# A gated linear attention block and a gated MLP on one core: the decay of the state once per 128 tokens instead of once per 64, its transport through device memory, a broadcast load of the bias, and a new order of steps

## The chip, the cores and the metric

The kernel runs on one core of a Trainium2 chip. The metric is device time in microseconds (us) from launch to end, as the median of several executions. The engines of the core work side by side, each through its own list of instructions in order: TensorE (PE; its weight loads are the row PEld), VectorE (DVE), ScalarE (ACT), GpSimd (POOL), and SyncE (SP), which here only issues DMAs.

## The reference

B = 4 batches, H = 8 heads, S = 768 tokens, D = 48 features a head. First a linear attention whose state decays by a gate per feature, then an MLP with spatial gating over the tokens and a residual:

```
f = sigmoid(f_logit)
for t in range(S):
    state = f[t][:, None] * state + outer(k[t], v[t])      # per batch and head, 48 x 48
    y[t]  = q[t] @ state
x = y as (B, S, 384)
h = gelu(x @ w_in)                 # 1024 columns: u is the first 512, v the last 512
v_n = (v - mean) / sqrt(var + 1e-6) * g_ln
v_s = einsum('ts,bsd->btd', w_sg, v_n) + b_sg[:, None]
out = x + (u * v_s) @ w_out
```

## The kernel before

The tokens are cut into 24 tiles n of 128 tokens, six to a batch. Inside a tile the attention works in two chunks of C = 64 tokens. With c the running sum of log f from the start of the chunk, the kernel scales q by exp(c) (step `mq`) and k by exp(-c) (`mk`); the scores of a chunk are then a masked product of the two, and the state is carried from chunk to chunk in scaled form. After each chunk the new products are added to the state (`sa`, `state_add`) and the sum is multiplied by the whole decay of the chunk, exp(c) of its last token (`sm`, `state_mul`). That decay stands along tokens-by-features and is wanted with features on partitions, so it has to be turned. For the six tiles of the first batch PE turns it (`do`, `dec_pick`, L544: eight small matmuls, which pick rows 63 and 127 of exp(c)), and DVE or ACT copies it out of PSUM (`di`, `dec_take`). For tiles 6 to 23 it goes through device memory: one DMA writes the two rows to `dec_d` (`do`, L532), two DMAs read them back, one for even heads and one for odd ones (`di`, L536), each element on its own partition.

The names of a tile's steps: `f`, `q`, `k`, `v` load inputs; `e`, `l` make log f on ACT; `cum` sums it with a triangular matrix (`tril`, L507, fp32, for the first batch; L510 and L511 in two fp32r parts after that); `up`, `dn` are the two exponentials; `tr` turns q and k with PE (L559, first batch), later tiles are turned by DVE and device memory (`tt`, `to`, `ti`); `tc` copies them; `w` copies v rows; `su` (`scores`, L604 scores and L609 state products, pair of heads by pair of heads); `ms` masks; `y` (L652) makes the output; `ty`, `jy` take it from PSUM; `xT` (L681), `xh`, `xl` turn and split x in a high and a low half; `hv` and `hu` are the products with w_in; `gv`, `ns` ... `nl` are gelu and the norm of v, whose split halves are `vh` and `vh_lo`; `sg` is the product over tokens with w_sg; `sb`, `sm_`, `sh`, `sl` add the bias, gate and split; `po` is the product with w_out; `re`, `out` add x and store. Every large product is three fp32r matmuls (high by high, high by low, low by high), all on L676. The weights arrive as float64 and are decoded in seven steps, `wa` to `wf` (one `ldin` or `ldout` load, then work on ACT, DVE and POOL); w_sg is turned by `wT` (L436).

The bias b_sg is one row of 768 numbers that every partition needs. Before, it is loaded to one partition (`b`), spread over 128 by two matmuls with a row of ones (`bb`, L909), and copied by ACT (`bc`) to `b_bc`.

What runs when is written out by hand: `ORDER` lists all steps, with an engine where there is a choice. A planner (`Plan.run`) walks the list with the costs in `T` and `W` to give every step a buffer, a PSUM bank and a planned start; on each engine the order is that of the list. Matmuls on zeros (L1054, `Plan.warm`) are put where the planner sees PE idle before 45 us, to keep its clock up.

Of the kernel before, what the change touches and what calls it, by code (L numbers as in the profile page):

```python
# [76 lines left out]
wT2.1 hv2 wh2.1 waout3 tc4.1 w4.0:ACT tc4.0 mq5:POOL w3.0:POOL wrin2 nl1 mk5 sa3.1 wcin2 wl2.1 y3 su4 ty3 gv2 wein0
sm3.1:POOL sa4.0 wpout3 ns2 tr5 bb1 do5 ldin3 ldsg0 ldout1 tc5.0:DVE ms4 tc5.1:DVE e6 jy3 di5 wfin1:POOL sm4.0:POOL
wfin0:POOL hu0.1 xT3 wT0.0 nd2 w4.1:POOL w5.1:POOL wdin2 sa4.1 wein2:DVE bc1 l6 lh6 wain3 y4 su5 wT0.1 xh3 w5.0:ACT
nd0 nq0 wh0.0 wqout3 wfin2 wpin3 xl3 wqin3 ms5 wh0.1 nq2 ty4 wl0.0 wl0.1 nr0 sm4.1:POOL nh0:DVE wrout3 sa5.0 jy4  # L80
waout1 gu0.1 sm5.0:POOL nr2 wpout1 nl0 hu0.2 hv3 xT4 y5 wT1.1 gu0.2 gv3 xh4 ty5 nh2 wh1.1 hu0.0 wqout1 wcout3 ll6
wrin3 jy5 xl4 ns3 wcin3 wdout3 xT5 hv4 nd3 xh5 nq3 q7 f7 ldout2 f8 ldout0 k7 wl1.1 xl5 wdin3:POOL sz6 nr3 hu1.0 hv5
nl2 waout2 gv4 wein3 wrout1 wcout1 wdout1 ns4 wfin3 weout3:DVE nd4:DVE nh3 nl3 weout1 v8 ldsg5 ldsg4 v6 v7 k6 q8 f9 q6
ldsg3 w8.0:ACT gv5 hu1.2 wfout1 wpout2 wqout2 ns5 nd5:DVE nq4 gu1.0 nr4 hu1.1 cum6 nq5 gu0.0 gu1.2 nr5 wfout3 wrout2
wcout2 nh4:DVE wdout2 nh5:DVE nl5 weout2:DVE nl4 gu1.1 up6 dn6 e7 l7 lh7 hu1.3 hu0.3 sg0.0 wT4.0 mk6 tt6.0 mq6 tt6.1
wfout2 ll7:POOL zr gu0.3 gu1.3 wh4.0 f10 to6 do6 cum7 sg0.2 wl4.0 sb0.0 sm_0.0 sb0.2 up7 dn7 e8 e9 ti6.0 ti6.2 ti6.3
ti6.1 k8 wT3.1 wT5.0 wT3.0 mq7:POOL mk7:POOL sg0.3 wh3.1 wh5.0 l8 wh3.0 lh8 wl3.1 tt7.0 tt7.1 wl5.0 wl3.0 sm_0.2:POOL
ll8:POOL cum8 wT4.1 wT5.1 l9 tc6.1 waout0 up8 dn8 lh9 sh0.2:DVE tc6.0:DVE sb0.3 sl0.2 wpout0 wqout0 ll9:POOL su6 wh5.1
wh4.1 sg0.1 ms6 wl4.1 mk8 wrout0 mq8 wl5.1 wcout0 cum9 di6.1 f11 di6.0 do7 to7 di7.1 ti7.2 di7.0 ti7.3 e11 up9 e10 dn9
l10 sh0.0 lh10 wdout0:POOL sb0.1 sa6.0 sm_0.1 weout0:DVE tt8.0 tt8.1 f12 ti7.1 k9 do8 ti7.0 q9 to8 sg1.0 sg1.2  # L90
wfout0:POOL mk9 sm6.0 sa6.1 ll10:POOL l11 sh0.1 tc7.1 sm_0.3 tc7.0:DVE sm6.1:POOL sl0.1 w6.0 sh0.3 w7.0:ACT w6.1:ACT
cum10 su7 y6 sl0.3 sl0.0 f13 di8.0 ti8.0 ti8.2 ti8.1 ti8.3 tt9.0 sb1.0 lh11 e13 ty6 up10 dn10 tc8.0 e12 tc8.1
ll11:POOL mq9:POOL jy6 tt9.1 sb1.2 ms7 sa7.0 sm7.0 w7.1 sa7.1 po1 po0 k10 to9 q10 di8.1 do9 v9 xT6 su8 y7 sm7.1 re0
xh6 ty7 po2 cum11 out0 ti9.3 di9.0 ti9.2 ti9.1 ti9.0 xl6 mk10 tt10.0 mq10:POOL jy7 sm_1.2 up11 sh1.2 ms8 sa8.0 tt10.1
sm8.0 w8.1:ACT w9.1:ACT dn11 sa8.1 re1 tc9.1:DVE sl1.2 sm_1.0 l12 tc9.0 hv6 xT7 y8 su9 k11 to10 q11 v10 ti10.1 di9.1
do10 k12 q12 f14 xh7 ty8 gv6 lh12 sh1.0:DVE mk11 sl1.0 ll12:POOL re2 jy8 xl7 tt11.0 mq11 sg1.1 xT8 cum12 sg1.3 xh8 l13
# [1077 lines left out]
```

## Time and profile before

| what | value |
|---|---|
| runs | 360.13, 360.68, 362.65 us; median 360.68 |
| span of the profiled execution | 358.9 us |
| outside the span, median less span | 1.8 us |
| granted TensorE clock, mean | 0.996 of full speed |
| busy: PE, PEld, DVE, ACT, POOL | 351.7, 322.9, 243.5, 213.7, 98.9 us |

The span runs from the first to the last instruction of the profiled execution, whose own time outside the profiler is not recorded; the median of the runs is 1.8 us above the span. Engine busy times overlap with one another. The ends of matmuls are modelled, so a PE that is shown as busy all the time may still have room; PEld, the weight loads, is a second witness.

### The profile page before, as it was taken

The numbers are of one execution on the slowest core, as the hardware profiler recorded it, in microseconds if no ns is written. First come the engines' busy times: TensorE is split into PE (matmuls) and PEld (weight loads), VectorE is DVE, ScalarE is ACT, GpSimd is POOL, SyncE is SP. The second block draws the span as 40 slices with busy tenths as digits, with TensorE's granted clock in tenths as the row PEclk, the third lists the DMA queues.
The fourth block names the chain that finished last, engine by engine and source line by source line (L and its number), as shares of the span: only waits on it lengthen the run. The fifth ranks groups of instructions, "written<-read, shape, count | busy, mean of one in ns | idle before, by whom it ended". The sixth has DMA issues, their size and how long they took to land.

```text
span 358.9 us, 11336 instructions
## 1 busy us (share of the span) xinstructions
PE 351.7 (98%) x4664; PEld 322.9 (90%) x4664; DVE 243.5 (68%) x553; ACT 213.7 (60%) x469; POOL 98.9 (28%) x158
## 2 busy tenths in 40 slices
PE   8999999999999999999999999999999999999994
PEld 3778788999999899999999999999998998999993
DVE  4888889969899956666655778457667665324551
ACT  5688799896737896996355758485226463701000
POOL 3433534243511140234122222114124121201210
PEclk9999999999999999999999999999999999999998
DMA  8999947955767867766357452742264440010012
GB/s 185 220 188 265 186 132 179 210 158 112 185 157 173 190 167 154 165 149 140 80 133 182 78 154 57 200 79 75 81 112 112 121 106 2 2 66 2 0 44 96
DMA packets 133903, 45.74 MB, mean 127 GB/s; under 512 B 117205, under 2 KB 130261, under 8 KB 133846
## 3 DMA queue, kind: packets, MB, share of 16 engines
q1 hardware_dynamic: 133846, 44.96, 55.0%
q8 instruction: 38, 0.62, 0.8%
q14 instruction: 19, 0.16, 0.1%
HBM read 33.09 MB, written 11.85 MB: 125 GB/s over the span
## 4 chain that ended last, share of the span: by engine, by line
PE 87%; DMA 5%; DVE 3%; SPq 2%; ACT 1%; issue 1%
PE ps_b L676 65%; PE ps_y L652 6%; PE ps_s L604 4%; DMA raw<-kq_d 3%; PE ps_s L609 2%; PE ps_b L681 2%; PE ps_b L559 2%; PE ps_b L544 1%; PE ps_b L436 1%; PE ps_b L1054 1%; DMA kq_d<-gg 1%; DMA gg<-in_moe_w_in_dram 1%; PE ps_b L507 1%; PE ps_b L510 1%; PE ps_b L511 1%
## 5 line engine op out<-in xcount | busy, mean ns | idle before, releaser
L676 PE MATMUL ps_b<-w_sg_hi,vh 128*128 128x384 f32 x192 | 65.6, 342 | 0.0
L676 PE MATMUL ps_b<-w_sg_hi,vh_lo 128*128 128x384 f32 x192 | 64.8, 338 | 0.0
L676 PE MATMUL ps_b<-w_sg_lo,vh 128*128 128x384 f32 x192 | 64.8, 338 | 0.0
L676 PE MATMUL ps_b<-w_out_hi,gg 128*128 128x384 f32 x174 | 48.2, 340 | 0.0
L769 DVE SCALAR_TENSOR_TENSOR tmp<-ps_b,cols,b_bc 128x384 f32<-128x384 f32 x32 | 19.4, 610 | 24.9 <-PE ps_b L676 24.7
L676 PEld LDWEIGHTS ps_b<-w_sg_hi,vh 128*128 128x128 f32 x192 | 36.0, 188 | 0.3
L676 PEld LDWEIGHTS ps_b<-w_sg_lo,vh 128*128 128x128 f32 x192 | 36.1, 188 | 0.0
L676 PEld LDWEIGHTS ps_b<-w_sg_hi,vh_lo 128*128 128x128 f32 x192 | 36.0, 188 | 0.0
L297 ACT ACT_TABLE_LOAD x27 | 34.6, 1283 | 0.5
L676 PEld LDWEIGHTS ps_b<-w_out_hi,gg 128*128 128x128 f32 x174 | 31.7, 188 | 0.3
L676 PE MATMUL ps_b<-w_out_lo,gg 128*128 128x384 f32 x87 | 29.1, 335 | 0.0
L676 PE MATMUL ps_b<-xTh,w_in_hi 128*128 128x384 f32 x84 | 29.0, 345 | 0.0
L676 PE MATMUL ps_b<-xTl,w_in_hi 128*128 128x384 f32 x84 | 28.4, 338 | 0.0
L676 PE MATMUL ps_b<-xTh,w_in_lo 128*128 128x384 f32 x84 | 28.4, 338 | 0.0
L652 PEld LDWEIGHTS ps_y<-vs,st 64*64 64x64 f32 x768 | 24.4, 134 | 4.2 <-issue 2.4
L774 POOL TENSOR_TENSOR tmp<-tmp,u 128x384 f32<-128x384 f32 x13 | 14.1, 1088 | 49.6 <-DVE tmp L769 37.2
L652 PE MATMUL ps_y<-vs,st 64*64 64x48 f32 x768 | 27.1, 219 | 0.0
L652 PE MATMUL ps_y<-S,sk 48*64 48x48 f32 x768 | 27.0, 219 | 0.0
L299 ACT ACTIVATE f<-f 128x384 f32<-128x384 f32 x48 | 25.1, 524 | 2.1 <-DMA f<-in_f_logit_dram 1.7
L676 PE MATMUL ps_b<-w_in_hi,xTh 128*128 128x512 f32 x63 | 25.5, 405 | 0.0
L633 POOL TENSOR_TENSOR S<-S,dec 112x192 f32<-112x192 f32 x22 | 12.5, 570 | 45.8 <-DVE S L630 34.2
L604 PEld LDWEIGHTS ps_s<-sk 48*64 48x64 f32 x768 | 20.8, 133 | 4.8 <-issue 2.1
(150 smaller groups left out, 889.7 us busy)
## 6 DMA issues: line engine op xcount, KB each, us to landing
kq_d<-gg SPq DMA_DIRECT2D x18, 384.0 KB, 2.5
f<-in_f_logit_dram SPq DMA_DIRECT2D x24, 192.0 KB, 3.5
kq<-in_q_dram SPq DMA_DIRECT2D x24, 192.0 KB, 4.3
kq<-in_k_dram SPq DMA_DIRECT2D x24, 192.0 KB, 4.1
vs<-in_v_dram SPq DMA_DIRECT2D x24, 192.0 KB, 4.5
raw<-kq_d SPq DMA_DIRECT2D x36, 128.0 KB, 2.5
out_dram<-tmp SPq DMA_DIRECT2D x24, 192.0 KB, 1.8
gg<-in_moe_w_in_dram SPq DMA_DIRECT2D x8, 384.0 KB, 5.5
```

What stands on the lines that cost most here:

```text
L297: nc.scalar.preload_act_table_set(SETS[want])
L299: nc.scalar.activation(dst, src, func, **kw)
L436: nc.tensor.transpose(ps[:, j], t[:, (hf * KT + j) * P : (hf * KT + j + 1) * P], ident)
L559: nc.tensor.transpose(psum[f"tr{n}"][j][:W2, p * P : (p + 1) * P], kq[:, j, 2 * p : 2 * p + 2, :].rearrange("t h d -> t (h d)")[:, :W2], i ...
L604: nc.tensor.matmul(ps_s[rows(score_rows(c, 2 * p + par)), par, p * C : (p + 1) * C], sk[r, 0, p, c], sk[r, 1, p, c], start=True, stop=True)
L609: nc.tensor.matmul(ps_s[feat(par), c, 256 + p * D : 256 + (p + 1) * D], kt[rows(c), h], vs[rows(c), h], start=True, stop=True)
L633: ENG[e].tensor_mul(state_to(n, c), state_to(n, c), decay(n, c))
L652: nc.tensor.matmul(ps_y[rows(c), half, h * D : (h + 1) * D], a, m, start=start, stop=stop)
L676: nc.tensor.matmul(ps, a, m, start=(j == 0), stop=(j == len(seq) - 1))
L681: nc.tensor.transpose(ps[:, j], x_sb[n][:, j * P : (j + 1) * P], ident)
L769: nc.vector.scalar_tensor_tensor(t, psum[f"sg{g}.{ft}"][:, :E], g_col[:, ft : ft + 1], b_bc[:, tokens(g)], op0=ALU.mult, op1=ALU.add)
L774: ENG[e].tensor_mul(t, t, uT.pop((g, ft)))
```

## The change

- The running sum starts anew only with each 128-token tile: the line that cleared the block of `tril` between the chunks is gone. exp(c) and exp(-c) now reach over 128 tokens.
- The state of chunk 0 is not decayed any more: `sa` of the first chunk adds (or, for a batch's first tile, copies), `sa` of the second adds, and one `sm` a tile multiplies. 40 multiplications become 20, as the last tile of a batch needs none. `y` of tile n waits for `sa` n.0 and `sm` n-1.
- The decay of a tile is one row of 384 numbers. All 24 tiles send it through device memory: `do` is one DMA, `di` two, with 4 instead of 8 numbers per partition. The PE steps `do` of tiles 0 to 5 and their copies are gone, and 18 DMAs come in their place on SP.
- The bias is loaded by one DMA that reads the row for each of 128 partitions; `bb`, `bc` and the row of ones are gone.
- `scores` makes the scores of three pairs of heads, their state products, then the scores and state products of the fourth, instead of alternating pair by pair.
- `ORDER` and the costs `T`, `W` are redone, with other choices of engine; due times, which nothing read, are gone.

```diff
-        pool.memset(tril[:C, C:], 0.0)
...
-        nc.gpsimd.memset(dec[:, NT:], 1.0)
+        nc.gpsimd.memset(dec, 1.0)
...
     def dec_out(n, e):
-        ENG[e].dma_start(dec_d[n].rearrange("c (h d) -> c h d", d=D), eb_of[n][C - 1 :: C, :, 0:D])
+        ENG[e].dma_start(dec_d[n : n + 1].rearrange("c (h d) -> c h d", d=D), eb_of[n][P - 1 : P])
     def dec_in(n, par, e):
-        ENG[e].dma_start(
-            dec[feat(par), n].rearrange("d c p -> d (c p)"),
-            dec_d[n].rearrange("c (p x d) -> x d (c p)", x=2, d=D)[par],
-        )
-    def dec_pick(n):
...
-    def dec_take(n, e):
...
+        ENG[e].dma_start(dec[feat(par), n], dec_d[n].rearrange("(p x d) -> x d p", x=2, d=D)[par])
...
+        for some in (range(NP - 1), range(NP - 1, NP)):
+            for p in some:
+                pair_scores(p)
+            for p in some:
+                pair_state(p)
...
-    def state_add(n, c):
+    def state_add(n, c, e):
         if n % NT == 0 and c == 0:
-            nc.vector.tensor_mul(state_to(n, c), U(n, c), decay(n, c))
+            copy(e, state_to(n, c), U(n, c))
         else:
             nc.vector.tensor_add(state_to(n, c), Sts[n % 2][:W2, c], U(n, c))
-    def state_mul(n, c, e):
-        ENG[e].tensor_mul(state_to(n, c), state_to(n, c), decay(n, c))
+    def state_mul(n, e):
+        ENG[e].tensor_mul(state_to(n, 1), state_to(n, 1), dec[:, n, :, None].to_broadcast((W2, NP, D)))
...
-    dma("b", lambda e: nc.sync.dma_start(b_bc[0:1], b_sg[None, :]), W["b"], ["f5"], due=35.0)
-    op("one", lambda e: nc.gpsimd.memset(one, 1.0), T["one"], ())
-    for g in range(2):
-        pe(f"bb{g}", lambda g=g: b_rows(g), T["bb"], ["b", "one"], due=40.0)
-        op(f"bc{g}", lambda e, g=g: copy(e, b_bc[:, tokens(g)], psum[f"bb{g}"][:, :E]), T["bc"], [f"bb{g}"], unbank=f"bb{g}")
+    dma("b", lambda e: nc.sync.dma_start(b_bc, b_sg[None, :].to_broadcast((P, S))), W["b"], ["f5"])
...
+        dma(f"do{n}", lambda e, n=n: dec_out(n, e), W["do"], [f"up{n}", f"mq{n}"], free=[("eb", f"up{n}", 0)])
+        for par in range(2):
+            dma(f"di{n}.{par}", lambda e, n=n, par=par: dec_in(n, par, e), W["di"], [f"do{n}", "clear"])
```

The start of `ORDER`, up to the first `hv`, before (-) and after (+):

```diff
-f0 ldin6 ldin1 cs clear f1 q0 k0 e0 l0 wain6 zy zs wpin6 wqin6 v0 q1 k1 ldin4 ldin7 v1 f2 cum0 f3 wain1 up0 dn0 e1
-wrin6 wpin1 wcin6 wqin1 wdin6 wein6 l1 mq0:POOL one wrin1 mk0 wcin1 cum1 tr0 up1 tc0.1 dn1 w0.0 tc0.0:DVE wain4
-w0.1:ACT wdin1:POOL wain7 do0 su0 mq1 wfin6:POOL ldin5 q2 k2 ms0 di0 sa0.0 sm0.0 mk1:POOL sz0 do1 tr1 sa0.1 sm0.1
-wpin4 wqin4 wrin4 di1:ACT tc1.0 tc1.1 y0 su1 w1.0:ACT e2 w1.1:ACT l2 ty0 e3 l3 wpin7 wcin4 wqin7 wrin7 wdin4 f4 q3 f5
-v2 k3 sa1.0 wcin7 jy0 ms1 sm1.0:POOL cum2 cum3 wdin7:POOL wain5 wpin5 wqin5 up2 up3 dn2 dn3 y1 xT0 ty1 xh0 e4 mq2
-wrin5 mk2 do2 wcin5 jy1 xl0 di2:ACT l4 mq3 tr2 xT1 wein7 tc2.1 xh1 e5 wdin5:POOL cum4 do3 tc2.0:DVE sa1.1 wein5 l5 up4
-di3:ACT su2 cum5 v3 ldin0 ldsg2 b ldsg1 q4 ldin2 q5 k4 ldout3 wfin7:POOL sm1.1:POOL w2.0:ACT w2.1:ACT dn4 xl1 cum_c
-wein4:DVE wfin5 mk3 wfin4 tr3 hv1 tc3.0 tc3.1 wain0 up5 dn5 gv1 ms2 sa2.0 sm2.0:POOL sa2.1 wpin0 sm2.1:POOL wqin0
...
+f0 cs ldin6 f1 clear e0 zy ldin7 ldin4 l0 wain6 wpin6 e1 l1 q0 cum_c wain7 wain4 k0 wqin6 ldin5 wrin6 cum0 wpin7 wcin6
+up0 wqin7 wpin4 dn0 zs mk0 f2 v0 wain5 wdin6 mq0:POOL wein6 wrin7 wqin4 do0 q1 wpin5 k1 wqin5 wrin5 wrin4 wcin7 wcin5
+cum1 tr0 e2 tc0.0 tc0.1 su0 l2 wcin4 cum2 up1 wdin5 mq1 v1 f3 wein5:DVE di0.0 di0.1 dn1 up2 f4 w1.1:ACT sa0.0 sa0.1
+wdin7 ms0 ldin1 w0.0:ACT mk1:POOL w0.1:POOL wdin4 tr1 tc1.0 sz0 do1 y0 wein4:DVE tc1.1 wfin5 k2 e3 q2 w1.0 ty0 sm0 q3
+zr su1 e4 jy0 l3 dn2 wain1 ms1 l4 xT0 sa1.0 wpin1 wein7:DVE mk2 wqin1 cum3 mq2 y1 up3 cum4 wfin6:POOL dn3 xh0 ty1 tr2
+wfin7 di1.1 v2 xl0 jy1 mq3:POOL di1.0 xT1 wrin1 tc2.1 tc2.0 f5 k3 do2 sa1.1 xh1 xl1 e5 ldin0 wfin4:POOL w2.1:POOL do3
+wcin1 up4 ldsg2 l5 su2 hv1 dn4 wain0 w2.0:POOL cum5 sm1 sa2.0 v3 ldsg1 mk3 ms2 up5 sa2.1 q4 dn5 tr3 y2 k4 tc3.0
...
```

After the first `hv` the list before goes on with `su3 y2`, two `wT`, `hv0 bb0 xT2 do4 tr4` ... to `hu1.3 hu0.3 sg0.0`; the list after with `su3`, two `wT`, `hv0 tr4 xT2` ... to `hu1.2 sg0.0 hu1.3` (PE steps only).

## Rows read from the trace of the kernel before

**Rows 1.** The page, head and busy time by engine (us, share, instructions).

```profile
span 358.9 us, 11336 instructions
...
PE 351.7 (98%) x4664; PEld 322.9 (90%) x4664; DVE 243.5 (68%) x553; ACT 213.7 (60%) x469; POOL 98.9 (28%) x158
```

**Rows 2.** Windows: length; busy PE, PEld, DVE, ACT, POOL (instructions); granted clock, DMA share, GB/s.

```profile
0.00:10.00 10.00, 8.43 (x17) 3.49 (x18) 4.59 (x12) 5.72 (x12) 4.46 (x20) 1.00 0.94 185
10.00:70.00 60.00, 59.56 (x1025) 49.88 (x1026) 53.91 (x129) 49.40 (x119) 24.21 (x40) 1.00 0.92 198
...
100.00:350.00 250.00, 249.70 (x3252) 236.89 (x3251) 159.03 (x360) 135.31 (x287) 57.47 (x87) 1.00 0.46 106
```

**Rows 3.** Chain that ended last, 0 to 60 us: start, us, what.

```profile
9.89 0.91 PE ps_b L507 x2
...
11.69 0.69 PE ps_b L544 x8
...
13.46 0.42 PE ps_b L1054 x2
...
27.69 0.54 PE ps_b L1054 x2
...
28.50 0.09 PE ps_s L609 x8
28.59 0.13 PE ps_s L604 x8
...
29.25 0.84 PE ps_b L507 x2
30.09 0.87 PE ps_b L559 x8
30.96 2.09 PE ps_b L676 x9
...
37.90 0.84 PE ps_b L909 x2
...
47.43 0.88 PE ps_b L544 x8
```

**Rows 4.** The same chain, its end.

```profile
353.88 0.56 DVE tmp L800
```

**Rows 5.** Timeline of DVE: first weight step, last weight step ahead of the first h matmuls.

```profile
5.79 0.36 DVE L394 TENSOR_SCALAR u<-u 128x384 uint32<-128x384 uint32 x1 [3.46 <-ACT u L389]
...
29.25 0.55 DVE L427 TENSOR_TENSOR w_in_lo<-u,w_in_hi 128x384 fp32r<-128x384 f32 x1
```

**Rows 6.** Timeline of DVE: the last low half of the first batch.

```profile
71.42 0.75 DVE L742 SCALAR_TENSOR_TENSOR vh_lo<-vg,vg_rs,vh 128x512 fp32r<-128x512 f32 x1
```

**Rows 7.** Timeline of PE: the first spatial matmuls, and the first that reads token tile 4.

```profile
72.78 0.34 PE L676 MATMUL ps_b<-w_sg_hi,vh 128*128 128x384 f32 x1
...
74.89 0.34 PE L676 MATMUL ps_b<-w_sg_hi,vh 128*128 128x384 f32 x1
```

**Rows 8.** Groups by line: busy us, mean ns, idle before and its releaser.

```profile
L633 POOL TENSOR_TENSOR S<-S,dec 112x192 f32<-112x192 f32 x22 | 12.5, 570 | 45.8 <-DVE S L630 34.2 <-ACT f L299 5.7 <-DMA dec<-dec_d 5.1
...
L633 DVE TENSOR_TENSOR S<-S,dec 112x192 f32<-112x192 f32 x18 | 7.5, 419 | 1.4 <-DMA dec<-dec_d 1.1
...
L676 PEld LDWEIGHTS ps_b<-w_in_hi,w_sg_hi 128*128 128x128 f32 x18 | 3.4, 188 | 0.7
```

**Rows 9.** DMA of the page: share of the queue; issues, KB each, us to landing.

```profile
q1 hardware_dynamic: 133846, 44.96, 55.0%
...
gg<-in_moe_w_in_dram SPq DMA_DIRECT2D x8, 384.0 KB, 5.5
```

**Rows 10.** Instructions on the tile dec: ns min/median/max; its DMAs.

```profile
L536 SPq DMA_DIRECT2D dec<-dec_d x36: 302/470/1525, 79.2 to 290.5; - x36
...
DMA to landing us min/median/max: 2.0/2.4/3.3
```

**Rows 11.** Waits of SP's queue: total, times, longest.

```profile
SPq L536 <- DMA dec_d<-eb: 7.9, 5, 2.5
```

More of the change, by code (lines that the diff above doesn't have):

```diff
@@ L77 @@
[L77 to L96, printed above, removed]
@@ L142 @@
-sm_6.1:POOL sh6.1:DVE sl6.3 sl6.1 sb6.0 sm_6.0:POOL sm_6.2 sh6.0:DVE sl6.0 sh6.2 sl6.2 sb7.3 sb7.2 sm_7.3 sm_7.2:POOL
-sh7.3 sl7.3 sh7.2:DVE sl7.2 po18 po19 po21 re19 ok re18 out18 out19 po20 po22 ok_s re20 ok_e re21 re22 po23 out20
-out21 out22 re23 hold out23
+f0 cs ldin6 f1 clear e0 zy ldin7 ldin4 l0 wain6 wpin6 e1 l1 q0 cum_c wain7 wain4 k0 wqin6 ldin5 wrin6 cum0 wpin7 wcin6
+up0 wqin7 wpin4 dn0 zs mk0 f2 v0 wain5 wdin6 mq0:POOL wein6 wrin7 wqin4 do0 q1 wpin5 k1 wqin5 wrin5 wrin4 wcin7 wcin5
@@ new lines @@
+nr5 wl0.1 k8 q8 nh5:DVE l7 up6 dn6 nl5 wcout2 ldsg3 e8 mq6 wdout2 e9 mk6 l8 lh7:DVE hu0.3 weout2:DVE ldsg5 hu1.1 tt6.0
+f10 gu0.3 wfout3:POOL hu1.2 tt6.1 ll7 sg0.0 hu1.3 sb0.0 gu1.1 wT3.0 w8.1:ACT gu1.2 cum7 lh8:DVE wfout2:POOL wT3.1
+gu1.3 up7 wh3.0 dn7 sm_0.0:POOL do6 ll8 to6 ti6.1 wh3.1 w7.0 mq7 mk7:POOL wl3.0 ti6.2 e10 di6.0 ti6.3 wl3.1 sg0.2 l9
+wT4.0 sb0.2 cum8 sg0.3 wh4.0 up8 ti6.0 wT5.1 tt7.0 f11 sm_0.2:POOL dn8 lh9 di6.1 di5.1 sh0.0 tt7.1 mq8 to7 waout0
+wT5.0 ll9:POOL do7 tc6.0 tc6.1 wh5.0 e11 wl4.0 wpout0 mk8 wqout0 f12 l10 sb0.3 ti7.0 wT4.1 ti7.1 wl5.0 tt8.0 ti7.3
@@ new lines @@
+wh5.1 sm_0.3:POOL l11 wrout0 tt8.1 wh4.1 ti7.2 wcout0 do8 su6 w7.1:ACT w6.0:ACT cum9 to8 lh10 wdout0 sa6.0 wl5.1
+ll10:POOL sh0.3 sa6.1 ms6 sg0.1 sh0.2 di7.0 k9 tc7.1 up9 wl4.1 q9 tc7.0 cum10 y6 weout0:DVE ti8.0 lh11:DVE e12 su7
+sm6:POOL ti8.1 sl0.3 ll11 sl0.0 sb0.1 wfout0 mq9:POOL q10 v9 ms7 cum11 dn9 mk9:POOL ty6 jy6 l12 lh12 tt9.0 ti8.2 k10
+do9 sm_0.1 f13 ti8.3 di8.1 up10 dn10 sa7.0 ll12:POOL sg1.0 w8.0:ACT tt9.1 sh0.1 di7.1 xT6 w9.1:ACT sl0.2 sl0.1
+mq10:POOL up11 sb1.0 to9 xh6 sa7.1 sm_1.0 e13 di9.1 dn11 tc8.1 mk10 do10 tc8.0:DVE di9.0 f14 ti9.3 e14 ti9.0 ti9.1
@@ L145 @@
+nl23 hu7.2 hu7.0 hu7.1 gu7.1 hu7.3 gu7.0 ok sg7.1 sg6.2 gu7.2 sb6.2 sg6.1 sg7.3 sb7.1 sb6.1 sm_6.1:POOL sm_6.2:POOL
+sh6.2:DVE sm_7.1 sh7.1 gu7.3 sg6.0 sg7.2 sg6.3 sh6.1 sl6.1 sl7.1 sb7.3 sl6.2 sb6.0 sg7.0 sm_7.3 sm_6.0 sh6.0:DVE sh7.3
+sb7.2 sl6.0 sb6.3 sm_6.3 sh6.3 sl6.3 sb7.0 sm_7.0 sm_7.2:POOL sh7.0 sl7.0 sl7.3 sh7.2:DVE sl7.2 po18 po19 po21 po20
+re18 re19 out19 ok_s out18 re20 po22 out20 po23 ok_e re21 re22 re23 out22 out21 out23 hold
 """
@@ L333, in gla_moe_kernel @@
     Sts = [cp.tile([P, 2, NP, D], F32, name=f"S{i}") for i in range(2)]
-    ebs = [cp.tile([P, H, HD], F32, name=f"eb{i}") for i in range(2)]
-    dec_d = dp.tile([N, 2, E], F32, name="dec_d")
+    ebs = [cp.tile([P, H, D], F32, name=f"eb{i}") for i in range(2)]
+    dec_d = dp.tile([N, E], F32, name="dec_d")
     kq_d = dp.tile([N, P // BL, BL, NBL, 2, NP * BL], F32, name="kq_d")
-    dec = cp.tile([W2, N, 2, NP], F32, name="dec")
+    dec = cp.tile([W2, N, NP], F32, name="dec")
     def make_consts():
@@ L600, in scores, with pair_scores @@
         last = n % NT == NT - 1
-        for p in range(NP):
+        def pair_scores(p):
             for par, c in ((0, 0), (1, 1), (0, 1), (1, 0)):
@@ L897, in gla_moe_kernel @@
-    t = T_SG
-    for u in order:
-        due[u] = t
-        t += cost(u)
-    op("cs", lambda e: make_consts(), T["cs"], (), due=-9.0)
-    op("cum_c", lambda e: nc.vector.tensor_copy(cum, cs[:, 128:256]), T["cum_c"], ["cs"])
-    dma("g", lambda e: nc.sync.dma_start(g_col, g_ln.rearrange("(n p) -> p n", p=P)), W["g"], ["f5"], due=30.0)
-    one = raw[0:1, 0, 0 : P // BL].rearrange("p a t -> p (a t)")
-    def b_rows(g):
-        nc.tensor.matmul(psum[f"bb{g}"][:, :E], one, b_bc[0:1, tokens(g)], start=True, stop=True)
```

245 lines of the change are left out of this document (94 added, 151 removed).

## The prediction

> **What bounds the kernel now.** I read the page first: PE is busy for 351.7 of 358.9 us [rows 1]. Since the ends of matmuls are modelled, the windows come next, with PEld beside PE. From 100 to 350 us PE is busy for 249.70 of 250 us and the weight loads for 236.89, at the full clock, while DVE works for 159 and ACT for 135 [rows 2]. That stretch is bound by PE alone, and time is only won there by giving PE less to do or by reaching it sooner. From 10 to 70 us PE is busy for 59.56 of 60 but the loads for only 49.88, and DVE is busy for 53.91 [rows 2]. The chain of waits shows what lies behind that. Between the first sum at 9.89 us and the first product with w_in (`hv1`) at 30.96 us, PE runs matmuls on zeros in six pieces, 0.42 us the first, 0.54 the last, 4.06 together; none follows [rows 3]. So until about 28 us PE waits for others, and from then on each step stands ready when PE comes to it. The chain ends with the last matmuls and one residual at 353.88 us, after which 5.0 us pass to the end of the span [rows 1, 4]. The start (9.9 us until real work) and this tail are not touched by the change.
>
> The share of the weight loads deserves a second look. In 10 to 70 us they fill 49.88/60 = 83%. But `hv1`, nine matmuls in 2.09 us with nothing waited for, has nine loads of 188 ns, 1.69 us or 81% [rows 3, 8]. A share of 83% therefore doesn't prove that PE is waiting. The Trainium skill (Perfetto Trace Analysis, Identifying the Most-Contended Engine) says that headroom on TensorE is judged by the share of weight loads and not by matmul time; taken alone it would put some 10 us of idle time into this stretch and make DVE its bound, which is the first rival below.
>
> **What PE loses.** Six `do` of eight matmuls are gone. On the chain they cost 0.69 us the first and 0.88 us the last, 4.52 us together; two `bb` cost 0.84 each, 1.68 us [rows 3]. Sum: 6.20 us. Nothing is added on PE. Four of the `do` (2.95 us) come before `hv1`, where PE waits for others anyway; two `do` and both `bb` (3.25 us) come after it, where PE doesn't wait.
>
> **Where the early part goes.** What `hv1` needs is the decoded right half of w_in and x of tile 1. PE itself could be there sooner: 30.96 less the zeros 4.06, less four `do` 2.95, less `cum5` 0.84 and `tr3` 0.87, which the new order puts behind `hv1` [rows 3], is 22.2 us. DVE can't follow so far. It begins with the weights at 5.79 us and ends the last of them at 29.80 [rows 5]. Counting the DVE steps of the list, 50 stand up to that point before; after the change 47 stand up to the last one that `hv1` needs. The difference is one step fewer each of `mk`, `mq`, `wc`, `di`, `sm`, two `tc` fewer, two `wd` and two `we` more. Steps of 384 elements take 0.55 us, 0.47 from start to start, so that this makes about 1.5 us less. With the same idle time on DVE `hv1` starts at about 29.80 - 1.5 = 28.3 us; if all idle time between (about 5 us by the same count) went, at 23.3. Loads speak for the upper half, as the same bytes are still ahead of `q3`; a shorter list of waits speaks for some gain. I take 27.5 us. Then PE has won 30.96 - 27.5 = 3.5 us, must make up `cum5` and `tr3` (-1.7), and saves 3.25 after it: 5.0 us. With the ends 28.3 and 23.3 it would be 4.2 and 9.2; the PE floor of 22.2 is below both.
>
> **Other parts.** (1) Half of the 40 `sm` go. They cost 570 ns on POOL (22) and 419 on DVE (18) [rows 8]; POOL and DVE are not the bound after 70 us [rows 2], so it counts there for nothing. Before 70 us the new list keeps as many on DVE as before, and POOL takes other work in their place. (2) 18 DMAs more on SP before 50 us. Such a DMA takes SP 0.30 to 1.5 us, in the middle 0.47, and lands after 2.0 to 3.3 us [rows 10]: 8.5 us of SP's time, in which only loads wait. `do` waits for `mq` and stands ahead of `q1`, `k1` and others; `di` waits for `do` to land, and behind them all stand the loads of the next tiles. Cover: each pair has other loads between, and DMA engines that hold a backlog (share 0.92 to 0.94, w_in landing 5.5 us after its issue [rows 2, 9]). I take nothing; without the cover it is the second rival. (3) Small packets: the queue's 133846 packets take 55.0% of 16 engines for 358.9 us [rows 1, 9], 23.6 ns each. Twelve `di` of 192 elements are at most 2304 packets, 3.4 us of all engines, and at least nothing; the wide load of the bias is 384 KB, 2.0 us at the 198 GB/s of that stretch [rows 2]. Tiles 6 to 23 lose the same kind of packets (18 times 192), where the share is 0.46. I take nothing, since `b` is first read behind the first `sg`, and since the share falls after 50 us; 5.4 us of transport is inside the second rival. (4) The new order in `scores`: a block of eight scores takes 0.13 us and one of state products 0.09 [rows 3]. The blocks stay the same. If the 0.04 between them were the price of each change of kind, four changes fewer in each of 24 tiles would be 3.8 us less; a longer wait of the mask for the last pair could cost as much as one block, 0.13 in 24 tiles, 3.1 us more. I take 0, as no wait stands between the blocks now. (5) The two copies of the bias and four of the six `di` leave ACT, two leave DVE; the two clears that fall away are on POOL. All beside PE. (6) The order after 70 us: PE had no idle time there to remove; a new one could come, since matrices and stores moved against each other. I take 0 and keep 1 us for the range.
>
> **The rivals.** *First: DVE becomes the bound before `sg0.0`.* The first product over tokens begins at 72.78 us, and reads token tile 4 at 74.89; the `nl` for it ended at 72.17 on DVE [rows 6, 7]. After the change `sg0.0` stands one `hu` (1.6 us) sooner in PE's list, and PE arrives 5 us sooner, so DVE has to be 3.9 us sooner than before (74.89 - 5.0 - 1.6 = 68.3 against 72.17). By the steps of the list it has 1.5 us less to do up to there, and it idles for 6.1 us between 10 and 70 [rows 2]. If that idle time stays, `nl` ends at 70.7, and PE stands 2.4 us: a gain of 2.6, 358.1 us. For it speaks DVE's 90%, against it that a part of DVE's idle time is waiting for PE and goes with it. *Second, slower: the decay's way through memory stops SP.* Where before `di` waited for `do`, SP stood for 7.9 us in five waits, 2.5 the longest, 1.6 on average [rows 11]. In the first batch each of six tiles has that pair, between the loads that feed everything. If each stops the loads for 1.6 us and no backlog hides it, 9.5 us come to the path: 360.7 - 6.2 + 9.5 = 364.0 us. It becomes a loss when the stops sum up to more than 6.2 us. The Trainium skill (DMA: Bandwidth & Descriptors, Rules for kernel authors) warns here that transfers under 64 KB pay mostly for overhead; the row agrees, 2.0 us or more for 1.5 KB, but this is latency, and it counts only where the state or SP waits for it. Against this rival: the list puts three to five other issues between each early `do` and its first `di`, and the multiplication is wanted only for the tile after. *Third: the idle time of DVE goes too*, `hv1` at 24.5 and nothing late behind it: 8 us gain, 352.7 us.
>
> **How the numbers follow.** The median 360.68 is 1.8 us above the profiled span [rows 1]; the sum is a difference of spans and is taken off the median: 360.68 - 5.0 = 355.7 us. Forecast (gain 3.8 to 6.8, 353.9 to 356.9): 0.60. Third rival (below 353.9): 0.10. First rival (356.9 to 360.5): 0.19. Second (above 360.5): 0.11. The range goes from 352.7, the third rival, to 359.8, which takes in the first and leaves out the second. A change of 1% is 3.6 us, about what a measurement of this kernel can tell from none, as the three runs lie 0.7% apart. Below 357.1: 0.60 + 0.10 and a little of the first rival, 0.71. Above 364.3: 0.06 of the second; within 1%: 0.23.
>
> **What would show it.** In the profile after: PE busy for some 5 us less in all, no L544 and L909, matmuls on zeros again before `hv1` and only there; `hv1` at 27 to 28 us; PEld from 10 to 70 us no lower than 83%. The first rival shows as PE or PEld waiting for DVE `vh_lo` ahead of `sg0.0` at 65 to 70 us; the second as SP waiting for `dec_d` in the first 40 us, with DMA share well under 0.9 and late `f`, `q`, `k`. The prediction is wrong if PE waits by more than 2 us after 70 us, which nothing in the profile before foretells, or if the planner's new costs put zeros in front of steps that are ready.

## The result and the profile after

The changed kernel takes 364.81 us (median of 17 runs, 363.14 to 369.17) where the kernel before, beside it, takes 360.68 (17 runs, 359.76 to 363.53). The ratio is 1.0105, with a 95% interval of 1.0081 to 1.0130. The forecast was 355.7 us in a range of 352.7 to 359.8: the change costs 4.1 us where 5.0 were to be gained. Side by side with the last two experiments it gave the same again, 364.98 us and 1.0106 (1.0064 to 1.0148).

Each ratio is to the kernel before run beside it, and can differ from the quotient of the two medians by up to 0.4%. One run of 571.95 us at a granted clock of 0.558 (old order, picks kept) and one of 369.17 us of the changed kernel are left out of the ratios, not out of the medians; all four runs of "picks twice" are in.

The profiled execution has a span of 366.8 us and took 368.5, at the upper end of the timed runs; a second one, of the repeated run, has 363.5. Where the two differ in what is argued from them, both are given.

The page of the changed kernel, head, busy time, the kinds of step in the chain of waits, and the queue. They answer to [rows 1] and [rows 9].

```profile
span 366.8 us, 11242 instructions
...
PE 350.8 (96%) x4620; PEld 318.7 (87%) x4620; DVE 247.1 (67%) x561; ACT 198.9 (54%) x437; POOL 99.0 (27%) x150
...
q1 hardware_dynamic: 129296, 45.31, 52.0%
...
PE 63%; DVE 13%; DMA 9%; ACT 6%; SPq 4%; issue 3%; POOL 0%; ACTq 0%; DVEq 0%; POOLq 0%
```

In the kernel before that last line was:

```profile
PE 87%; DMA 5%; DVE 3%; SPq 2%; ACT 1%; issue 1%
```

The work that was to go is gone: 48 matmuls of `do` and 4 of `bb` fewer, 8 on zeros more, which makes 4664 - 44 = 4620. But a quarter of the chain that PE filled before now runs through DVE, loads, ACT and SP. The windows, columns as in [rows 2], show where:

```profile
10.00:70.00 60.00, 56.68 (x982) 45.92 (x981) 56.64 (x131) 48.93 (x114) 26.87 (x37) 1.00 0.94 203
...
100.00:350.00 250.00, 244.92 (x3210) 229.63 (x3210) 156.28 (x355) 120.86 (x259) 57.78 (x86) 0.99 0.42 103
```

From 10 to 70 us PE is busy 2.9 us less than before and the loads of weights 4.0 us less, 77% of the stretch, while DVE is busy 2.7 us more. So about half of what was taken off PE's list became idle time there; some of the rest is zeros. From 100 to 350 us PE lost 4.8 us that it did not lose before [rows 2].

Next the milestones. These are rows of the chain around `hv1`, as in [rows 3], with the chain's end, as in [rows 4], and then the timeline of PE at the first spatial matmul, as in [rows 7]:

```profile
28.34 0.57 PE ps_s L581 x24
...
29.40 2.27 PE ps_b L658 x9
...
361.85 0.56 DVE tmp L782
```

```profile
71.28 0.33 PE L658 MATMUL ps_b<-w_sg_hi,vh 128*128 128x384 f32 x1
```

`hv1` begins at 29.40 us in the chain (30.96 before) and `sg0.0` at 71.28 (72.78 before). In the new list `sg0.0` stands one `hu` of 1.6 us sooner, so like for like the changed kernel is at 72.9 us there: nothing has been won. From there to the last residual it takes 361.85 - 71.28 - 1.6 = 289.0 us, where the kernel before takes 353.88 - 72.78 = 281.1 [rows 4, 7]. In the second profiled execution these two figures are 72.2 and 286.1. All of the loss lies behind `sg0.0`. Most of it can be seen on PE itself: from 72 to 352 us PE is idle for 0.3 us in the kernel before and for 5.6 us in the changed one (4.4 in the second profile). In the profile shown the granted clock also falls to 0.50 around 121 us, which costs some 1.7 us (an estimate: the shares of full clock missing in the windows from 120 to 124 us, 0.35, 0.50, 0.50 and 0.35).

What stalls there is seen best at the longest wait of PE after 70 us. First the timeline of PE, then that of ACT and DVE around it, all of the changed kernel:

```profile
117.13 0.34 PE L658 MATMUL ps_b<-w_sg_hi,vh_lo 128*128 128x384 f32 x1
120.01 0.67 PE L663 MATMUL ps_b<-cs,x 128*128 128x128 f32 x3 [2.54 <-DVE x L642]
...
118.17 0.62 ACT L300 COPY sk<-raw 112x512 f32<-112x512 f32 x1 [7.05 <-DMA raw<-kq_d]
118.69 0.47 ACT L638 COPY x<-ps_y 128x384 f32<-128x384 f32 x1
...
118.19 0.43 DVE L300 COPY sk<-raw 112x512 f32<-112x512 f32 x1 [2.23 <-DMA raw<-kq_d]
118.53 0.68 DVE L599 TENSOR_TENSOR st<-ps_s,cs 128x512 f32<-128x512 f32 x1
...
119.40 0.55 DVE L642 SCALAR_TENSOR_TENSOR x<-ps_y,x 128x384 f32<-128x384 f32 x1
```

ACT stands for 7.05 us before the copy of tile 10's turned pieces (`tc10.0`), DVE for 2.23 before its twin. Tile 10 is not urgent. But behind the copy on ACT stands `ty8`, and behind the other on DVE `jy8`, and these two make the `x` that PE waits for. Each engine takes its list in order, so a copy written ahead of its landing stops whatever is written behind it. The chain shows the transfers that were late, kq_d to memory and back, 4.75 and 4.69 us:

```profile
106.75 4.75 DMA kq_d<-gg
...
113.37 4.69 DMA raw<-kq_d
```

The page of before has a median of 2.5 us for either. Such waits can be summed for the whole stretch from 72 to 356 us. These are waits of ACT and POOL for loads of f, q and k and for the turned pieces (`raw`), total, times and longest, first of the kernel before, then of the changed one:

```profile
ACT sk L304 <- DMA raw<-kq_d: 5.6, 3, 4.2
ACT sk L304 <- DMA kq<-in_q_dram: 0.7, 1, 0.7
...
POOL kq L524 <- DMA kq<-in_k_dram: 5.1, 2, 3.0
POOL kq L529 <- DMA kq<-in_q_dram: 5.0, 1, 5.0
```

```profile
ACT f L295 <- DMA f<-in_f_logit_dram: 14.2, 6, 4.8
ACT sk L300 <- DMA raw<-kq_d: 10.5, 5, 7.0
...
POOL kq L522 <- DMA kq<-in_q_dram: 38.7, 8, 11.3
POOL kq L517 <- DMA kq<-in_k_dram: 16.7, 3, 8.8
POOL ll L491 <- DMA raw<-kq_d: 8.5, 1, 8.5
POOL tmp L756 <- DMA raw<-kq_d: 5.7, 1, 5.7
```

With those of DVE (2.3 and 7.9) they make 18.7 us before and 102.2 after. Waits for the loads of v are not in these sums; they are 12.0 and 2.1 us. Two of the rows after, 14.2 us together, belong to steps that don't read `raw` (`ll` and `sm_`), so what held them is open. These engines are off the path most of the time, so most of this costs nothing, but it says how closely the redone order stands behind its loads. The kernel's planner books 1.3 us of landing for every load, behind its transport.

### The profile page after: what moved, and what is told of

Its sections match the earlier page's. It is cut to its first block, busy times and chain, and to the rows that moved or that the text cites. A ratio compares the mean times of both kernels' runs of the same rounds, so it can differ in the third digit from the quotient of the medians.

```text
span 366.8 us, 11242 instructions
## 1 busy us (share of the span) xinstructions
PE 350.8 (96%) x4620; PEld 318.7 (87%) x4620; DVE 247.1 (67%) x561; ACT 198.9 (54%) x437; POOL 99.0 (27%) x150
## 2 busy tenths in 40 slices
DMA packets 129353, 46.09 MB, mean 126 GB/s; under 512 B 112504, under 2 KB 125584, under 8 KB 129296
## 3 DMA queue, kind: packets, MB, share of 16 engines
q1 hardware_dynamic: 129296, 45.31, 52.0%
## 4 chain that ended last, share of the span: by engine, by line
PE 63%; DVE 13%; DMA 9%; ACT 6%; SPq 4%; issue 3%; POOL 0%; ACTq 0%; DVEq 0%; POOLq 0%
PE ps_b L658 53%; PE ps_y L634 3%; DMA f<-in_f_logit_dram 3%; DMA kq<-in_k_dram 3%; DMA raw<-kq_d 2%; PE ps_s L581 2%; ACT L293 2%; SPq L560 2%; PE ps_b L663 1%; DMA kq_d<-gg 1%; PE ps_s L588 1%; ACT f L295 1%; DVE vh_lo L724 1%; DVE u L391 1%; DVE u L404 1%
## 5 line engine op out<-in xcount | busy, mean ns | idle before, releaser
L756 POOL TENSOR_TENSOR tmp<-tmp,u 128x384 f32<-128x384 f32 x15 | 16.2, 1084 | 62.4 <-DVE tmp L751 55.3
L522 POOL TENSOR_TENSOR kq<-kq,eb 128x384 f32<-128x384 f32 x15 | 16.1, 1073 | 54.4 <-DMA kq<-in_q_dram 47.7
L638 ACT COPY x<-ps_y 128x384 f32<-128x384 f32 x24 | 11.6, 482 | 35.2 <-PE ps_y L634 32.6
L658 PE MATMUL ps_b<-w_out_lo,gg 128*128 128x384 f32 x87 | 29.4, 338 | 0.0
```

What stands on the lines that cost most here:

```text
L522: ENG[e].tensor_mul(qt, qt, eb_of[n])
L638: nc.scalar.copy(x_sb[n], ps_y[:, 0, 0:E])
L658: nc.tensor.matmul(ps, a, m, start=(j == 0), stop=(j == len(seq) - 1))
L756: ENG[e].tensor_mul(t, t, uT.pop((g, ft)))
```

## Experiments

Two theories stood at the start. The *order theory*: the mechanisms gain about what was forecast, and the redone order of the steps loses it. Its sharper form is the *landing theory*: the order stands too close behind its loads. The *early-memory theory*: the six early decays' way through device memory loses, whatever the order. A third was added for the missing gain, that the stage up to `sg0.0` is held by loads and VectorE right behind TensorE.

**Old order, new mechanisms, picks kept.** Decay per tile, paired scores and the broadcast bias in the order of before; the early decays are still picked out by PE:

```
 ORDER = (order of before, without bb*, bc*, one, sm*.0; sm{n}.1 becomes sm{n}, ahead of sa{n+1}.0)
-dma(f"do{n}", dec_out) ... dma(f"di{n}.{par}", dec_in)      # n < 6
+pe(f"do{n}", dec_pick)     # ident[:, P - 2 : P], last row used
+op(f"di{n}", dec_take)
```

> The changed kernel's state (one decay per tile, bias by the broadcast DMA, scores paired as changed) with the step order of before, and the six early decays still picked out on TensorE (one row of the tile, where before took two). Order theory (the mechanisms gain what was forecast, the redone order loses it): 354 to 357.5 us, sg0.0 at 70 us or a little before. Early-memory theory (the six early decays' way through device memory is what loses, whatever the order): 355 to 358 as well, since that way is not taken here. Third theory, that the decay per tile gains nothing because the early stage waits for its loads and not for VectorE: 359.5 to 361.5.

Measured: 361.09 us, ratio 0.9975 (0.9900 to 1.0049). One decay per tile, the pairs of scores and the bias by DMA gain nothing that shows by themselves, so the first half of the order theory, that the mechanisms gain what was forecast, falls here. (PE is lighter by the two `bb` alone, 1.7 us. The profile of this kernel is of the run of 571.95 us, and is not used.)

**The same, early decays through memory.**

```
-q1 k1 ldin4 ldin7 v1 f2 f3 ldin5 q2 k2 ...                            # SP; picks on PE
+q1 ldin4 k1 ldin7 do0 f2 v1 di0.0 di0.1 f3 do1 ldin5 k2 q2 ...
```

> As the run before it, but the six early decays go through device memory as in the changed kernel, with their DMAs (and some early loads) put where the kernel's own planner had least waiting; otherwise the step order of before. Order theory: 354.5 to 358 us. Early-memory theory: 361 us or more, with TensorE's steps before hv1 2 us and more behind those of the run with picks.

Measured: 359.63 us, 0.9953 (0.9894 to 1.0011). The early-memory theory asked for 361 and more and falls: with its DMAs issued early enough, the way through memory costs nothing that shows. But 6.2 us less work on PE gains hardly more than 1.7 did. One reason can be read in the trace: the planner, which fills the gaps it sees with zeros, put 42 matmuls on zeros here and 28 in the kernel before. Behind 10 us they stand for 9.7 us against 4.7 (sums of their groups in the timeline, an estimate), so that some 5.0 of the 6.2 us came back as filler.

**New order, picks kept.**

```
 ORDER = (the changed one)
-do0 ... di0.0 di0.1 (SP)
+do0 (PE) di0 (DVE), and so on for n < 6
```

> The changed kernel with its redone order, but the six early decays picked out on TensorE again (one row each, about 3 us of TensorE work) and no early decay DMAs. Order theory: 362 to 367 us, no better than the changed kernel. Early-memory theory: 357 to 360 us.

Measured: 365.87 us, 1.0128 (1.0066 to 1.0190). Without any early decay DMA the new order is as slow as with them. The loss is in the order.

**New order to 70 us, old order from there.**

```
 ORDER = changed[: index of "gu1.1"] + [step of before's order if not yet placed],
         some 350 steps behind the seam shifted, most by up to 30 places
```

> The changed kernel with its redone order up to gu1.1 (about 70 us) and from there the order of before, smoothed over the seam. If the loss comes from the order after 70 us (7.5 of the 13.9 us of TensorE time lost against before, in the two traces, lie there): 357 to 360 us. If it comes from the early stage: 362 to 366 us, as the changed kernel.

Measured: 364.78 us, 1.0116 (1.0041 to 1.0191). This came out against the expectation for a loss after 70 us. The trace says that it didn't test it: of the new early part nothing is late at `sg0.0` (70.32 us), but behind the seam, from 85 to 125 us, ACT waits 5.8 us for `raw` and 3.3 for `f`, and the stretch behind `sg0.0` takes 285.1 us like for like, with PE idle for 3.4 us from 72 to 352. I take it that the seam made waits of its own; no run shows it apart.

**Few zeros.** The first kernel with a planner that fills gaps with matmuls on zeros up to 12 us only:

```
-steps = plan.warm(plan.run(), 45.0, ...)
+steps = plan.warm(plan.run(), 12.0, ...)
```

> The first run again (old order, decay per tile, bias by DMA, early decays picked on TensorE), but without the multiplications by zeros planned after 12 us. If the saved TensorE work turned into zeros that stand ahead of steps that were ready: 356.5 to 358.5 us. If the stage to 70 us follows VectorE and the loads, and the zeros only fill gaps: 359 to 361 us, as with them, and TensorE shows idle time in their place.

Measured: 359.77 us, 0.9967 (0.9939 to 0.9996). The zeros alone don't eat the gain. `hv1` starts at 29.22 us, 1.5 sooner than before by the timeline (30.72), and all of it is given back ten microseconds later. This is the timeline of PE at `tr4`, and of DVE just ahead:

```profile
39.73 1.10 PE L548 MATMUL ps_b<-cs,kq 128*112 128x128 f32 x4 [1.93 <-DVE vg_mv L710]
...
38.64 1.03 DVE L517 TENSOR_TENSOR kq<-kq,f 128x384 f32<-128x384 f32 x1 [1.05 <-DMA kq<-in_k_dram]
```

`mk4` stood until `k4` had landed, and PE stood 1.93 us for `mk4`. (The wait is put down to `vg_mv`, the last DVE step counted; the `kq` product beside it is what `tr4` reads.) The test has a price of its own: without zeros the granted clock falls to between 0.50 and 0.68 from 39 to 43 us, 1.7 us by the same sum as above. The two other kernels with few zeros, below, lose 1.7 us each in the same way, from 14 to 19 and from 26 to 30 us.

**Picks twice.** The kernel before, with each early pick issued twice:

```
-for p in range(NP):
+for p in [*range(NP)] * 2:      # in dec_pick
```

> The kernel before with the 24 matmuls of the six early decay picks issued twice each round (the same values written again), 4 to 4.5 us more TensorE work, most of it in the first 46 us. If TensorE sets the end of every stage, as the prediction had it: 364 to 365.5 us. If the stage to 70 us follows VectorE and the loads: 360 to 362 us.

Measured: 371.22 us, 1.0276 (1.0197 to 1.0354), the four runs from 366.05 to 374.70. The profiled one, the 366.05, has `sg0.0` at 77.45 us, 4.7 later than before, and 281.1 us from there as before. So PE does bound the early stage against more work, with hardly any slack. Adding 4.5 us costs 4.7; taking 6.2 us of real work away, in the old order with the way through memory, brought 0.8 at `sg0.0` (71.98 us). That would fit two limits on top of each other, PE and what it waits for; but 5.0 of those 6.2 us had come back as zeros, so the second limit rests on the waits at `tr4`, above and below, and not on this pair of runs. (The four times go with the granted clock: 366.05 us at 0.998, 368.68 at 0.985, 373.75 at 0.977, 374.70 at 0.974. Why it is lower in three of them is open.)

**New order, rearranged for later landings.** The order up to about 40 us is kept; in the rest steps were moved at random, and a move was kept where the kernel's planner, told of later landings, ended no later:

```
-LAND = 1.3
+LAND = 2.2      # while rearranging
```

> The changed kernel; its order up to about 40 us is kept, the rest of the order is rearranged by the kernel's own planner with loads that land 0.9 us later than it assumed (352 of 1510 steps move by more than 8 places); computation and early decays as changed. Landing theory (the redone order puts ScalarE's, VectorE's and GpSimd's steps so close behind their loads that real landings stall these engines in order): 357 to 361 us, with less waiting of ScalarE for f. If the loss is in the early order or in the mechanisms: 363 to 366 us.

Measured: 361.63 us, 1.0020 (0.9997 to 1.0042). Most of the loss is gone, with the same early order and the same mechanisms.

**Old order, rearranged in the same way.** `LAND = 2.2` again, from the first experiment's order.

> The first run's kernel (old order, early picks on TensorE) with its order rearranged in the same way for later landings. Landing theory: the old order has room behind its loads already, so little is to be had: 357.5 to 360 us. If its rest of 33 us of TensorE waiting could go: 354 to 357 us.

Measured: 362.63 us, 1.0050 (1.0020 to 1.0081), which neither theory had. Rearranging by the planner is no improvement in itself: on the old order it lost 0.75% against the kernel of the first experiment, though the two intervals overlap.

**One pair moved back.**

```
-... ti10.1 f15 su9 y8 q12 tt11.1 tc10.0 tc10.1:DVE ms9 ... v10 do12
+... ti10.1 f15 su9 y8 q12 tt11.1 ms9 ... v10 tc10.0 tc10.1:DVE do12
```

> The changed kernel with one pair of steps moved: the two copies of tile 10's turned q and k (tc10.0 on ScalarE, tc10.1 on VectorE) stand behind xh7 and xl7, as they did in the order of before, and no longer ahead of ty8 and jy8. In the changed kernel's trace ScalarE stood 7.05 us and VectorE 2.23 us before these copies for the raw pieces to land, with ty8 and jy8 queued behind them, and TensorE lost 2.82 us at xT8. Landing theory: 1.5 to 2.8 us under the changed kernel, 362 to 363.5 us, and xT8 without a wait. If a later wait takes its place, or the early order is the cause: 364 to 366 us.

Measured: 363.57 us, 1.0091 (1.0066 to 1.0116). In the profile the stall at `xT8` is gone and the stretch behind `sg0.0` takes 284.4 us in place of 289.0 and 286.1; the ratio tells it from the changed kernel by 0.15% at most, less than the intervals (the quotient of its medians, 363.57 to 361.17, is 1.0066, so it may have given back more). The stall is one of several, and in the second profile of the changed kernel another stood in its place (1.7 us of PE at `su13`).

**k4 earlier.** One change to the kernel with few zeros, on SP alone:

```
-q4 ldin2 q5 k4
+q4 k4 ldin2 q5
```

> The run with few zeros again (old order, decay per tile, early picks), with the load of k4 issued ahead of ldin2 and q5: three issues of the SP queue change places, nothing else. In that run TensorE stood 1.93 us at tr4 for mk4, which waited for k4 to land at 38.6. If loads are the bound right behind TensorE to 70 us: tr4 starts up to 1.9 us earlier and the run takes 0.5 to 1.9 us less, 358 to 359.3 us. If VectorE bounds the stage: no change, 359.5 to 360 us.

Measured: 361.11 us, 1.0009 (0.9977 to 1.0040): no gain. The trace shows both at work, loads and DVE. PE at `tr4`, and DVE ahead of it:

```profile
39.79 0.97 PE L548 MATMUL ps_b<-cs,kq 128*112 128x128 f32 x7 [2.20 <-DVE vg_mv L710]
...
38.31 0.36 DVE L387 TENSOR_SCALAR u<-u 128x384 uint32<-128x384 uint32 x1 [1.77 <-ACT u L382]
...
39.18 0.55 DVE L517 TENSOR_TENSOR kq<-kq,f 128x384 f32<-128x384 f32 x1
```

Now `k4` is there, but the load of w_in that had to give way (`ldin2`) isn't, and DVE stands for that, 1.77 us, with `mk4` behind it. `tr4` starts at 39.78 us in the kernel before, 39.87 in the changed one, 39.73 with few zeros and 39.79 here, but at 38.22 in the second profile of the changed kernel and at 39.15 to 39.65 in its rearranged forms. What holds the stretch is not the same in the two orders. In the chains of the two kernels with few zeros and picks, loads fill 12.9 and 17.9 us of the 30 from 10 to 40 us, and DVE 2.1 and 1.5. In the chain of the changed kernel DVE fills 39.9 us of the 60 from 10 to 70 us, PE 10.0, and no load stands in it behind that of `k0`, which lands at 10.95. (These are sums of the rows of each chain.)

**Old order, memory, few zeros.** The memory way at the places of the picks: `do0` after `f3`, `di0` after `k2`; zeros to 12 us; `k4` early.

```
+f3 do0 ldin5 q2 k2 di0.0 di0.1 f4 ...
```

> Old order, decay per tile, bias by DMA and the early decays through device memory (their issues after f3 and k2 and so on, at the places where the picks stood), without zeros after 12 us and with k4 ahead of ldin2. It has some 3 us less TensorE work in the first 46 us than the run before it. If TensorE's work before hv1 counted: 355.5 to 357.5 us. If the stage follows loads and VectorE: 358 to 360 us, as the run before it.

Measured: 362.39 us, 1.0056 (1.0024 to 1.0087), beyond both theories. Its chain around 20 us shows the second rival of the prediction, in one place:

```profile
20.27 3.58 DMA dec<-dec_d
...
23.98 0.37 DVE S L613
...
26.40 1.96 PE ps_y L632 x64
```

Issued behind `q2` and `k2` at 18.74 and 20.2 us, the decay lands at 23.85; DVE stands for it, `ms1` stands behind on DVE, and PE loses 4.69 us before `y1`. In the changed kernel `do0` goes out ahead of `q1` and `k1`, and nothing of the kind is seen.

**The new order with more room, twice, beside the changed kernel.** Rearranged again, this time from the load of `f6` on (about 35 us), with the planner's landings 0.6 to 1.3 us later than 1.3, from two random starts.

> The changed kernel itself once more, side by side with the two runs after it on the same chip. All theories: 364 to 366 us, 1.0 to 1.3% over the kernel before.

> The changed kernel; its order is kept up to the load of f6 (about 35 us), and the rest is rearranged by the kernel's own planner for loads that land 0.6 to 1.3 us later than it assumed (516 of 1510 steps move by more than 8 places); computation and early decays as changed. Landing theory: 357 to 361 us, at or under the kernel before and at least 3 us under the changed kernel beside it. If the early order or the mechanisms lose: 363 us or more.

> The same from another random start of the rearranging (520 steps move by more than 8 places), to see whether the result hangs on one lucky order. Landing theory: 357 to 361 us. If the run before this one was luck: the two differ by 3 us or more.

Measured: 364.98, 360.96 and 360.59 us; ratios 1.0106 (1.0064 to 1.0148), 1.0003 (0.9981 to 1.0025) and 0.9993 (0.9971 to 1.0015). Both come back to the time of before. The waits of ACT and POOL in the last one, 72 to 356 us:

```profile
ACT sk L299 <- DMA raw<-kq_d: 3.6, 2, 2.5
ACT f L294 <- DMA f<-in_f_logit_dram: 0.9, 1, 0.9
...
POOL kq L521 <- DMA kq<-in_q_dram: 23.0, 6, 6.0
POOL kq L516 <- DMA kq<-in_k_dram: 10.5, 4, 5.5
```

The profiled executions together. "To `sg0.0`" is the start of that step; for the kernels with the new order up to there 1.6 us for the one `hu` is added to it and taken off "behind", which runs to the start of the last residual. "Waits" are those of ACT, POOL and DVE for f, q, k and raw from 72 to 356 us, "for v" those for the loads of v. "PE idle" is the time from 72 to 352 us in which PE is not busy.

| kernel | to `sg0.0` | behind | waits | for v | PE idle | ratio |
|---|---|---|---|---|---|---|
| before | 72.8 | 281.1 | 18.7 | 12.0 | 0.3 | 1 |
| old order, memory | 72.0 | 281.0 | 21.1 | 7.7 | 1.4 | 0.9953 |
| few zeros | 72.9 | 281.2 | 22.0 | 9.4 | 1.2 | 0.9967 |
| k4 earlier | 71.5 | 281.5 | 17.1 | 9.7 | 1.6 | 1.0009 |
| old order, memory, few zeros | 75.6 | 279.7 | 18.1 | 8.9 | 0.0 | 1.0056 |
| picks twice | 77.5 | 281.1 | 23.4 | 15.6 | 0.3 | 1.0276 |
| old order, rearranged | 72.7 | 286.4 | 29.4 | 6.1 | 4.7 | 1.0050 |
| changed | 72.9 | 289.0 | 102.2 | 2.1 | 5.6 | 1.0105 |
| changed, again | 72.2 | 286.1 | 90.5 | 0.9 | 4.4 | 1.0106 |
| new order, picks | 73.4 | 284.4 | 86.0 | 1.5 | 2.9 | 1.0128 |
| one pair back | 72.1 | 284.4 | 76.6 | 0.5 | 3.1 | 1.0091 |
| new, then old | 71.9 | 285.1 | 28.4 | 5.8 | 3.4 | 1.0116 |
| new, rearranged | 71.2 | 283.2 | 39.9 | 16.4 | 1.3 | 1.0020 |
| new, more room | 71.7 | 282.5 | 48.5 | 25.4 | 1.2 | 1.0003 |
| new, more room, 2 | 71.5 | 282.1 | 38.2 | 4.7 | 0.6 | 0.9993 |

Six kernels with the old later order take 279.7 to 281.5 us behind `sg0.0`, whatever was done ahead of it; the new order takes 284.4 to 289.0, and 282.1 to 283.2 once it has room. Three rows don't fit the landing theory as the whole story. "New, then old" and "old order, rearranged" have few waits for loads and are slow behind `sg0.0` all the same. "New, more room" has, with v counted, 73.9 us of waits, about as many as "one pair back" with 77.1, and yet the time of before. PE's own idle time fits them all: up to 1.6 us of it stands with 279.7 to 283.2 us behind `sg0.0`, 2.9 us and more with 284.4 to 289.0.

## Why the prediction was wrong

*What bounds the kernel.* Right for 100 to 350 us in the kernel before. For 10 to 70 us the prediction rested on a chain that runs through PE, and held that PE waits only until 28 us. The chain did so at least in part because matmuls on zeros and picks filled PE's list; an engine that is given filler is busy where it would wait. That share of 83% for the weight loads was argued away with one `hv1`. By the Trainium skill's rule (Perfetto Trace Analysis, Identifying the Most-Contended Engine), on the share of weight loads, this stretch had room and PE was not its bound. The traces agree with it against the prediction in that PE, with 6.20 us of real work less, stood idle for 3.3 us from 10 to 70 us in the changed kernel; they speak against it in that adding 4.5 us to PE cost 4.7.

*What PE loses.* 6.20 us of real work, right in kind and size: the 52 matmuls are gone. "Nothing is added on PE" was not right, as the zeros behind 10 us grew from 4.7 to 6.4 us (an estimate, by the same sums as above).

*Where the early part goes: the first step that failed.* `hv1` was put at 27.5 us, within 23.3 to 28.3. It starts at 29.4 (28.7 in the second profile by the timeline), beyond the upper bound. The chain of the changed kernel shows why:

```profile
4.98 5.97 DMA kq<-in_k_dram
...
26.81 1.12 DVE u L395
27.93 0.27 DVE S L612
...
33.83 0.56 DVE u L391
...
58.51 0.49 DVE x L642 x2
...
67.04 0.75 DVE vh_lo L724
...
69.08 0.48 DVE w_sg_lo L859
...
69.61 6.55 PE ps_b L658 x36
```

`k0`, with `ldin7` and `ldin4` moved ahead of it on SP (and `ldin1` behind it), lands at 10.95 us, so that `mk0` starts at 11.04 where it started at 9.93 before, and from there to `su2` at 28.34 the chain is DVE's alone. The term "saves 3.25 after it" failed outright: it took PE to be free of waits behind `hv1`, and DVE stood right behind. From 33.2 to 59.0 us the chain is DVE's again but for 1.4 us of ACT, and the waits of PE for another engine from 10 to 72 us, 3.4 us together, are all for DVE. In the old order with few zeros it was `k4` or `ldin2` that held DVE, and DVE that held PE, at 39.8 us. Like for like the gain at `sg0.0` is 0 to 0.6 us in the changed kernel, and at most 1.6 in any of the runs, in place of 5.0.

*The order after 70 us: the second step that failed.* "I take 0 and keep 1 us for the range". It cost 7.9 us in one profile and 5.0 in the other; in the times, the changed kernel against its rearranged forms on the same chip, 4.0 and 4.4 us. The prediction had named this as what would prove it wrong, PE waiting by more than 2 us after 70 us, and it did (2.54 us at `xT8` alone). It saw that nothing in the trace of before foretold a wait, and took that for a sign of none. Yet the order was what the diff changed most, and the idle time of 0.3 us that PE has in the trace of before, from 72 to 352 us, is what the old order was worth. The new one leaves 5.6 us there, and 4.4 in the second profile.

*Other parts.* SP's 18 more DMAs were taken at nothing, and in the changed kernel that holds: SP waits for `dec_d` 3.1 us in 3 for the whole run, against [rows 11], none of it before 60 us. The bias, the packets and the score order show no price that these runs could tell. The count of packets had a slip: tiles 6 to 23 lose 36 times 192 of them, two `di` a tile, and not 18 times. With the 2304 of the early tiles that makes 4608 fewer, and the page has 4550 fewer (129296 against 133846). Three more of the signs named did not come: PE is busy for 0.9 us less in all and not 5 (350.8 against 351.7), PEld from 10 to 70 us fell to 77%, and zeros stand behind `hv1` as well, 1.1 us at 34.2 and 36.0 us.

*The rivals.* The first put DVE in PE's place before `sg0.0`. The stage and the engine were right, as the chain above shows; its size was not, as it left a gain of 2.6 us. Its marker, `vh_lo`, stands in the chain at 67.04 us, though what PE waited for, 0.6 us, was a decoded weight (`w_sg_lo`) behind it on DVE. The second, the decay's way through memory, does not happen in the changed kernel and does happen where the same DMAs are issued later, 4.69 us at `y1`. The third, more than forecast, has nothing for it. The case that made the loss, a new order that puts waits where there were none, had no chance of its own.

*What stays open.* Shown: the loss sits in the order behind the first 35 to 40 us, since three rearranged orders with the same mechanisms and early steps take it back. Supported, not settled: that room behind the loads is what they gave back. The waits fall from 102 to 38 to 49 us with it, but the planner moved some 350 to 520 steps at once, the single pair tells no time apart, and three rows of the table speak against that sum as the price of an order. Nor is it shown what made PE wait in each of the slow kernels; loads were followed back for the longest wait alone. The new early order was not joined to the old later one without a seam; by the table (71.2 to 72.9 us to `sg0.0`, 281.1 behind) an estimate is 0 to 1.6 us under the kernel before. No version here is shown to beat it: the lowest ratio, 0.9953, has 1 within its interval, and the one interval that lies under 1, that of few zeros (0.9939 to 0.9996), does so barely, while the same kernel with one load moved has 1.0009. And whether less work on PE before 70 us is worth anything was not tried without zeros in its place or a fall of the clock.

## What to carry to other kernels

An engine that is kept busy with filler looks like the bound, so count the filler apart; add work to it and take work away, and see to it that nothing fills the place of what was taken. Here adding moved the time, and the 6.2 us that were taken away came back as 5.0 us of zeros. When a change comes with a new static order, price the order first. The price is the idle time of the engine that bounds the stage, 0.3 us before and 5.6 after; where it comes from is found by following its longest waits back, as a step written ahead of a late landing stops everything written behind it on its engine. A sum of all engines' waits for loads (18.7 and 102.2 us) says where to look, and not what it costs.
